# A chunked scan and a routed expert layer: every engine of the scan in a fixed order, routing in smaller groups

## The chip, the cores and the metric

The kernel runs on one core of one Trainium2 chip. A core has five engines that run side by side, each with an instruction queue of its own that it works through in order: PE (TensorE, matrix multiplies; PEld in the tables is its weight load), DVE (VectorE), ACT (ScalarE), POOL (GpSimd) and SP (SyncE, which here only issues transfers). The metric is the device time of one execution in microseconds; lower is better.

## The reference

Two blocks in a row. The first is a state-space scan over 4 batches, 8 heads and 768 positions (head width 32, state width 16); the second takes its output as 3072 tokens of width 256 and sends each to one of 8 experts.

```python
for c in range(nc):                       # along the sequence, per batch and head
    cum = np.cumsum(log(a_chunk)); L = exp(cum_i - cum_j) * causal
    y[chunk] = ((C @ B.T) * L) @ x + (C @ state) * exp(cum)
    state = exp(sum(log a)) * state + sum(B * x * exp(cum_last - cum))
x = y as (3072, 256)
logits = normalize(x) @ normalize(expert_emb).T / tau
e = argmax(logits);  gate = softmax(logits)[e]
out[token] = gate * (relu(x[token] @ w1[e]) @ w2[e])
```

## The kernel before

**Tiling.** The sequence is cut into 6 chunks (`c`) of 128 positions. A unit is one batch of one chunk (all 8 heads); two units make a **pair** `p`, so that there are 12 pairs, two for a chunk. The scan is a software pipeline over steps `i` from -2 to 13: step `i` prepares pair `i+2` (B' and its transpose, the scaled C), makes the masked products of pair `i` (`inner`), the outputs of pair `i-1` (`outputs_before` from the states, `outputs_within` from the products), and turns pair `i-2` into rows by token together with its logits (`finish`, `keep_tokens`).

**Decays.** `decays` computes running products of `a` for chunks 0 to 3 (`kk` = 0) and 4 to 5 (`kk` = 1), scales for C in `f` and for B in `r`; `turn_decays` transposes `r` to `rT`. `scale_b` makes B' (`bp`) for a whole chunk, `scale_c` makes `cp` (DVE) and its two masked copies `cm` (ACT). `between` gets the decay from one chunk to the next by a scan over all 768 positions of a second copy of `a`; `spread_between` lays it out by four small multiplies and makes `blocks`, from which POOL builds the state weights `T` (four a chunk).

**Routing.** For each chunk, four units at once, `pick` finds the best expert of every token (six small DVE operations on the logits in `yt`), `place` counts with ones-matrices on PE how many tokens came before and writes the row number `row_of`, and POOL sends the four units' rows to a table `rows` in DRAM by four indirect transfers (a **scatter**). The last 160 rows of each expert's window of 416 are filled with ones first, by eight transfers from `none`.

**Experts.** Afterwards `moe` loads each expert's 416 rows (`xg`, issued by SP once all scatters have landed), multiplies up (`hp`), down (`yp`), and scatters the results to the output. Weights have three buffers; the first three experts' weights are loaded during the scan.

**Order.** The order on PE is the order of the code. On the other four engines a planner sets it at build time, by readiness as it estimates it; so the constants, the fills and the scan of `between` stand early there.

```python
        with tc.manual_schedule(engines={PE}):
            build_consts(k)
            route_consts(k)
            mamba(k)
```

Of the kernel before, what the change touches and what calls it, by code (L numbers as in the profile page):

```python
# [15 lines left out]
PE = mybir.EngineType.PE  # L16
# [8 lines left out]
KD, KF = DM // 128, F // 128  # L25
TR, NT = 104, 4
# [19 lines left out]
def build_consts(k):  # L46
    nc, pool = k.nc, k.const
    k.ident = pool.tile([128, 128], F32, name="ident")
# [40 lines left out]
def load_decays(k):  # L89
# [8 lines left out]
    k.a1 = k.mc.tile([NB * NH, S], F32, name="a1")  # L98
    nc.scalar.dma_start(k.a1[:], a)


def clip(k, v):
    k.nc.vector.tensor_scalar(out=v, in0=v, scalar1=1e-6, scalar2=1.0, op0=ALU.max, op1=ALU.min)


def decays(k, kk):
# [4 lines left out]
    clip(k, a)  # L111
    at = k.mc.tile([128, 1], F32, name=f"at{kk}")
    nc.vector.tensor_copy(out=at[:], in_=a[:, HQ : HQ + 1])
    nc.vector.memset(a[:, 0:Q:HQ], 0.0)
    nc.vector.tensor_tensor_scan(out=f, data0=a, data1=k.heads[:], initial=0.0, op0=ALU.mult, op1=ALU.add)
    w = k.mc.tile([128, 2], F32, name=f"w{kk}")
    tt(out=w[:, 0:1], in0=f[:, HQ - 1 : HQ], in1=at[:], op=ALU.mult)
    nc.vector.reciprocal(out=w[:, 1:2], in_=w[:, 0:1])
    nc.vector.reciprocal(out=r, in_=f)
    nc.vector.tensor_scalar_mul(r[:, 0:HQ], r[:, 0:HQ], w[:, 0:1])  # L120
    nc.vector.tensor_scalar_mul(f[:, 0:HQ], f[:, 0:HQ], w[:, 1:2])
# [9 lines left out]

def between(k):

    nc = k.nc
    a = k.a1
    clip(k, a[:])
    at = k.mc.tile([NB * NH, NC], F32, name="at")
    nc.vector.tensor_copy(out=at[:], in_=a[:, HQ:S:Q])
    nc.vector.memset(a[:, HQ:S:Q], 0.0)
    one = k.mc.tile([NB * NH, S], F32, name="one")  # L140
    nc.vector.memset(one[:], 0.0)
    nc.vector.memset(one[:, HQ:S:Q], 1.0)
    p = k.mc.tile([NB * NH, S], F32, name="p")
    nc.vector.tensor_tensor_scan(out=p[:], data0=a[:], data1=one[:], initial=0.0, op0=ALU.mult, op1=ALU.add)
    k.g = k.mc.tile([NB * NH, NC - 1], F32, name="g")
    nc.vector.tensor_tensor(out=k.g[:], in0=p[:, Q + HQ - 1 : S : Q], in1=at[:, 1:], op=ALU.mult)


def spread_between(k):
# [15 lines left out]
def expert_emb(k):  # L165

    nc = k.nc
    k.en = k.mc.tile([E, DM], F32, name="emb")
    nc.scalar.dma_start(k.en[:], k.emb)
    tau = k.mc.tile([E, 1], F32, name="tau")  # L170
    nc.scalar.dma_start(tau[:], k.tau.to_broadcast([E, 1]))
    sq = k.mc.tile([E, DM], F32, name="emb_sq")
    r = k.mc.tile([E, 1], F32, name="emb_r")
    nc.scalar.activation(sq[:], k.en[:], ACT.Square, accum_out=r[:])
    nc.gpsimd.tensor_tensor(out=r[:], in0=r[:], in1=k.half[0:E, 0:1], op=ALU.pow)
    nc.vector.tensor_scalar_add(r[:], r[:], 1e-6)
    nc.vector.tensor_tensor(out=r[:], in0=r[:], in1=tau[:], op=ALU.mult)
    nc.vector.reciprocal(out=r[:], in_=r[:])
    nc.vector.tensor_scalar_mul(k.en[:], k.en[:], r[:])
# [327 lines left out]


def place(k, c):

    nc = k.nc
# [363 lines left out]
```

## Time and profile before

| | us |
|---|---|
| Time of three runs | 334.68, 338.02, 339.41; median 338.02 |
| Profiled execution: time | 335.96 |
| Profiled execution: span | 334.2 |
| Start to the first `inner` product | 0 to 25.98 |
| Then to the end of `outputs_within` of pair 1 | to 42.53 |
| Then to the end of `outputs_within` of pair 11 | to 106.33 |
| Then to the issue of the first expert's rows | to 119.58 |
| Experts | 119.58 to 334.2 |

The span runs from the first to the last instruction; the profiled execution's time is 1.76 us more than it. Instructions have a start, a length and, in brackets, how long their engine stood idle before them and which event ended that. "PEclk" in a table is the granted share of TensorE's clock, 1.00 being 2.4 GHz and 0.50 1.2 GHz.

### The profile page before, as it was taken

How to read it: one execution, taken by the hardware profiler on the slowest of the kernel's cores; microseconds unless marked ns; L12 is line 12 of the kernel's file. 1: busy time of each engine (PE TensorE's matmuls, PEld its weight loads, DVE VectorE, ACT ScalarE, POOL GpSimd, SP SyncE). 2: the span in 40 equal slices, each digit the busy share in tenths (PEclk: the TensorE clock that was granted, in tenths of full speed). 3: DMA queues.
4: the chain of work that ended last, by engine and by line, in shares of the span. 5: the costliest groups of instructions: out<-in, count | busy, mean ns of one | idle time of the engine just before them, and what ended most of it. 6: DMA issues, size and time to landing. Idle time of an engine off the chain costs nothing.

```text
span 334.2 us, 4458 instructions
## 1 busy us (share of the span) xinstructions
PE 278.9 (83%) x1687; PEld 173.4 (52%) x1687; DVE 125.7 (38%) x371; ACT 66.6 (20%) x177; POOL 86.0 (26%) x107
## 2 busy tenths in 40 slices
PE   0439999999877019999999999999999999999930
PEld 0235788668656015555555555555555555555510
DVE  7815777456540615214214214214224114123030
ACT  2012253224312016121121031031121001011000
POOL 8202314453340713013114014014014004013040
PEclk9999999799797757999999999999999999999985
DMA  6899824010110252234415414514523001001010
GB/s 210 307 361 338 325 69 128 35 56 16 69 50 20 100 142 54 70 112 151 142 63 158 170 28 160 185 34 143 180 69 106 0 0 43 2 0 51 0 40 14
DMA packets 17871, 35.09 MB, mean 105 GB/s; under 512 B 2054, under 2 KB 10451, under 8 KB 17848
## 3 DMA queue, kind: packets, MB, share of 16 engines
q1 hardware_dynamic: 14168, 26.74, 24.4%
q0 software_dynamic: 2688, 6.50, 6.2%
q10 hardware_dynamic: 992, 1.55, 1.2%
q8 instruction: 14, 0.23, 0.3%
q14 instruction: 9, 0.07, 0.1%
HBM read 26.89 MB, written 8.14 MB: 105 GB/s over the span
## 4 chain that ended last, share of the span: by engine, by line
PE 59%; issue 20%; DMA 11%; DVE 5%; POOL 1%; ACTq 1%; ACT 1%; POOLq 0%; SPq 0%; DVEq 0%
PE hp L626 19%; PE yp L640 17%; DMA out_dram<-yo,to 8%; PE pg L308 6%; PE pz L362 4%; PE py L344 2%; PE py L330 2%; PE pf L252 2%; DMA rows<-none 2%; PE xt L617 2%; PE ot L654 1%; PE pf L270 1%; POOL out_dram L657 1%; DMA xg<-rows 1%; DVE g L314 1%
## 5 line engine op out<-in xcount | busy, mean ns | idle before, releaser
L626 PE MATMUL hp<-xT,w 128*128 128x416 f32 x256 | 97.3, 521 | 0.0
L640 PE MATMUL yp<-hT,w 128*128 128x416 f32 x256 | 90.8, 513 | 0.0
L640 PEld LDWEIGHTS yp<-hT,w 128*128 128x128 f32 x256 | 48.1, 190 | 38.5 <-issue 38.5
L626 PEld LDWEIGHTS hp<-xT,w 128*128 128x128 f32 x256 | 47.2, 193 | 32.9 <-issue 31.6
L657 POOL DMA_INDIRECT out_dram<-yo,to x32 | 32.2, 1006 | 91.5 <-DVE yo L656 84.8
L632 DVE TENSOR_SCALAR hT<-hp 128x416 f32<-128x416 f32 x32 | 18.9, 591 | 40.7 <-PE hp L626 27.5
L630 ACT ACTIVATE hT<-hp 128x416 f32<-128x416 f32 x32 | 16.6, 518 | 84.1 <-PE hp L626 61.4
L537 POOL DMA_INDIRECT rows<-yt,row_of x24 | 23.4, 976 | 30.5 <-issue 21.1
L314 DVE TENSOR_TENSOR g<-pg,mask 128x1024 f32<-128x1024 f32 x24 | 28.2, 1219 | 6.5 <-PE pg L308 6.5
L596 POOL TENSOR_TENSOR gr<-gr,half 104x4 f32<-104x4 f32 x8 | 8.3, 1036 | 75.9 <-ACT sq L592 75.9
L291 POOL TENSOR_TENSOR T<-V,blocks 128x256 f32<-128x256 f32 x20 | 12.6, 653 | 41.0 <-DVE blocks L159 14.6
L308 PE MATMUL pg<-cm,bt 32*128 32x256 f32 x192 | 21.8, 479 | 1.2 <-issue 0.9
L362 PE MATMUL pz<-turn,yT 128*128 128x136 f32 x96 | 17.5, 336 | 5.9 <-ACT yT L354 5.9
L362 PEld LDWEIGHTS pz<-turn,yT 128*128 128x128 f32 x96 | 14.8, 229 | 10.2 <-ACT yT L354 7.0
L656 DVE TENSOR_SCALAR yo<-ot,gate 104x256 f32<-104x256 f32 x32 | 15.4, 480 | 11.5 <-PE ot L654 11.5
L617 PE MATMUL xt<-ident,xg 104*128 104x104 f32 x64 | 7.8, 269 | 13.3 <-DMA xg<-rows 13.3
L647 DVE COPY yoT<-yp 128x416 f32<-128x416 f32 x8 | 4.7, 592 | 36.8 <-PE yp L640 26.1
L592 ACT ACTIVATE sq<-xg 104x256 f32<-104x256 f32 x32 | 12.9, 404 | 17.9 <-DMA xg<-rows 17.7
L654 PEld LDWEIGHTS ot<-ident,yoT 128*104 128x104 f32 x64 | 6.9, 130 | 16.6 <-DVE yo L656 8.5
L308 PEld LDWEIGHTS pg<-cm,bt 32*128 32x128 f32 x192 | 13.3, 220 | 4.4 <-issue 3.8
L645 ACT COPY yoT<-yp 128x416 f32<-128x416 f32 x8 | 4.1, 506 | 56.9 <-PE yp L640 56.9
L584 DVE TENSOR_REDUCE gm<-xg 104x4 f32<-104x32 f32 x8 | 1.5, 182 | 37.0 <-DMA xg<-rows 37.0
(147 smaller groups left out, 236.9 us busy)
## 6 DMA issues: line engine op xcount, KB each, us to landing
w<-in_moe_w_dram SPq DMA_DIRECT2D x16, 1024.0 KB
xg<-rows SPq DMA_DIRECT2D x8, 442.0 KB
x<-in_x_dram SPq DMA_DIRECT2D x6, 512.0 KB
b<-in_B_dram SPq DMA_DIRECT2D x6, 256.0 KB
ct<-in_CT_dram SPq DMA_DIRECT2D x6, 256.0 KB
rows<-none ACTq DMA_DIRECT2D x8, 170.0 KB
out_dram<-yo,to POOLq DMA_INDIRECT x32
rows<-yt,row_of POOLq DMA_INDIRECT x24
```

Of the source, the lines that this page charges most:

```text
L308: nc.tensor.matmul(k.pg[:, q, 256 * i : 256 * i + 256], lhsT=s.bt[r, i, :], rhs=s.cm[r, i], start=True, stop=True, tile_position=(32 * q, 0),)
L314: nc.vector.tensor_tensor(out=g[:], in0=k.pg[:, :, 256 * i : 256 * i + 256].rearrange("p q (t i) -> p q t i", t=2), in1=k.mask[:].unsqueez ...
L362: k.nc.tensor.matmul(k.pz[:, i, at : at + Y1], lhsT=yT[:, 2 * i + j, :], rhs=k.turn[:, j, :], start=(j == 0), stop=(j == 1), skip_group_ch ...
L537: d = nc.gpsimd.indirect_dma_start(out=k.rows[:, :], out_offset=bass.IndirectOffsetOnAxis(ap=row[:, b : b + 1], axis=0), in_=k.yt[:, NB * ...
L592: nc.scalar.activation(sq[:], s.x[:, i, :].rearrange("p (j w) -> p j w", j=KD)[:, :, 0:128], ACT.Square, accum_out=r[:, i : i + 1],)
L617: nc.tensor.transpose(t[:, i, :], s.x[:, i, Y1 * j : Y1 * j + 128], k.ident[:tr, :tr])
L626: nc.tensor.matmul(t[:], lhsT=s.w1[:, j, 128 * f : 128 * f + 128], rhs=s.xT[:, j, :], start=(j == 0), stop=(j == KD - 1))
L630: nc.scalar.activation(s.hT[:, f, :], t[:], ACT.Relu)
L632: nc.vector.tensor_scalar_max(s.hT[:, f, :], t[:], 0.0)
L640: nc.tensor.matmul(t[:], lhsT=s.w2[:, f, 128 * j : 128 * j + 128], rhs=s.hT[:, f, :], start=(f == 0), stop=(f == KF - 1),)
L656: nc.vector.tensor_scalar_mul(y[:], t[:tr, :], s.gate[:, i : i + 1])
L657: d = nc.gpsimd.indirect_dma_start(out=k.out[:, :], out_offset=bass.IndirectOffsetOnAxis(ap=s.to[:, i : i + 1], axis=0), in_=y[:], in_offs ...
```

## The change

- All engines of the scan now follow the order of the code; constants and the routing constants get places in it (`build_consts` first, `route_consts` in step 1).
- The fills move from ACT's queue to SP's, into step 1; the loads of the first weights move from step 1 to step 2 and stand behind the chunk loads there.
- The expert embedding is finished in step 1 instead of step -1.
- B' is made for one pair at a time, at the end of the step before its use.
- The decay from chunk to chunk comes from columns that `decays` already has (`finish_decays`), and the scan over 768 positions, with its own copy of `a`, goes.
- The state update is four combined operations for a chunk instead of two, into a new buffer each time; POOL's `T` are issued as `next_states` at a later place, from 12 buffers instead of 8.
- Routing groups: chunks 0 to 2 stay whole, chunks 3 to 5 are routed by pair (nine groups instead of six). Counting carries a running row, so that a group needs 3 or 5 small multiplies on PE instead of 5 to 10.
- Scatters: tables say in which step which group is picked (`PICK`), located (`PLACE`) and scattered (`SCATTER`), mostly two transfers a step; a second half first copies one element of the outputs of pair `i-2`, the others set one element.

```diff
+GROUPS = [(c, 0, NB) for c in range(3)] + [(c, b, 2) for c in range(3, NC) for b in (0, 2)]
 def decays(k, kk):
...
+def finish_decays(k, kk):
+    nc.vector.reciprocal(out=w[:, 1:2], in_=w[:, 0:1])
+    nc.vector.tensor_scalar_mul(f[:, 0:HQ], f[:, 0:HQ], w[:, 1:2])
+    nc.vector.tensor_tensor(out=w[:, 2:3], in0=w[:, 0:1], in1=at[:, 0:1], op=ALU.mult)
+    nc.vector.tensor_scalar_mul(k.parts[:, 0, kk, :], k.block[:], f[:, Q - 1 : Q])
+    nc.vector.tensor_scalar_mul(k.parts[:, 1, kk, :], k.block[:], w[:, 2:3])
...
 def between(k):
-    nc.vector.tensor_tensor_scan(out=p[:], data0=a[:], data1=one[:], initial=0.0, op0=ALU.mult, op1=ALU.add)
...
+        nc.tensor.matmul(
+            ps[:, 16 * b : 16 * b + 16], lhsT=k.spread[:, b, :], rhs=k.parts[:].rearrange("p v k g -> p (v k g)"),
...
 def states(k, c):
+        nc.vector.scalar_tensor_tensor(
+            out=V[:, b, :], in0=k.V[c - 1][:, b, :], scalar=k.whole[:, b, c - 1 : c], in1=st[:, b, :], op0=ALU.mult,
+            op1=ALU.add,
+        )
...
+        if i == 1:
+            fill_rows(k)
+        if i in (2, 4, 7):
+            load_weights(k, len(k.w1t))
+        for g in PLACE.get(i, ()):
+            locate(k, g)
+        if new is not None:
+            scale_c(k, new)
+        if 0 <= i < NP:
+            inner(k, i)
+        for g, u, n in SCATTER.get(i, ()):
+            scatter(k, g, u, n, done)
+        if i == 1:
+            next_states(k, 0)
+        elif i % 2 == 0 and 2 <= i and i // 2 < NC - 1:
+            next_states(k, i // 2)
...
+        for g in PICK.get(i, ()):
+            pick(k, g)
+        if new is not None and new + 1 < NP:
+            scale_b(k, new + 1)
         if i == -1:
             decays(k, 1)
+            finish_decays(k, 1)
+        if i == 0:
+            turn_decays(k, 1)
+            between(k)
+        if i == 1:
             turn_emb(k)
-        if i == 1:
-            turn_decays(k, 1)
-        if i % 2 and i >= 3:
-            pick(k, (i - 3) // 2)
-    place(k, NC - 1)
+            route_consts(k)
+    last = len(GROUPS) - 1
+    locate(k, last)
+    scatter(k, last, 0, 2, None)
+    count(k)
+PICK = {4: [0], 6: [1], 7: [2], **{p + 2: [p - 3] for p in range(6, 12)}}
+PLACE = {5: [0], 7: [1], 8: [2], **{p + 3: [p - 3] for p in range(6, 11)}}
+SCATTER = {
+    5: [(0, 0, 2)], 6: [(0, 2, 2)], 7: [(1, 0, 2)], 8: [(1, 2, 2), (2, 0, 2)], 9: [(2, 2, 2), (3, 0, 2)],
+    **{p + 3: [(p - 3, 0, 2)] for p in range(7, 11)},
+}
+def scatter(k, g, first, n, behind):
+    for u in range(first, first + n):
+        if u == first > 0:
+            nc.gpsimd.tensor_copy(out=k.tick[:], in_=k.yT[behind][0:1, 0, 0:1])
+        else:
+            nc.gpsimd.memset(k.tick[:], 0.0)
+        d = nc.gpsimd.indirect_dma_start(
```

ACT's queue at the start, before (`emb_sq` prepares the embedding, `none` is the tile of ones that the fills write to `rows`).

```order
L174 ACT_TABLE_LOAD
L174 ACTIVATE emb_sq,emb_r<-emb 8x256
L129 COPY rT<-pz 128x128
L242 COPY bt<-pz 128x256
L483 DMA rows<-none 80x544 x8
L262 ACTIVATE cm<-cp,tmask 128x2x128 x2
```

ACT's queue at the same place, changed.

```order
L169 ACT_TABLE_LOAD
L169 ACTIVATE emb_sq,emb_r<-emb 8x256
L123 COPY rT<-pz 128x128
L260 ACTIVATE cm<-cp,tmask 128x2x128 x2
L240 COPY bt<-pz 128x256
```

The fills are gone from between the first transposed B' (`bt`) and the first masked copies (`cm`), and `cm` stands ahead of `bt`.

DVE's queue at the start, before: from the long scan of `between` to the first B' (each of the last two rows one chunk).

```order
L144 SCALAR_TENSOR_TENSOR p_229<-a1_180,one_226 32x768
L117 TENSOR_TENSOR w1_302<-f_168,at1_298 128x1
L119 RECIPROCAL r_169<-f_168 128x128
L146 TENSOR_TENSOR g_231<-p_229,at_223 32x5
L118 RECIPROCAL w1_302<-w1_302 128x1
L120 TENSOR_SCALAR r_169<-r_169,w1_302 128x64
L121 TENSOR_SCALAR f_168<-f_168,w1_302 128x64
L220 TENSOR_TENSOR bp_219<-b_183,rT_170 128x16x16 x2
L220 TENSOR_TENSOR bp_258<-b_202,rT_170 128x16x16 x2
```

DVE's queue, changed: the second set of decays (chunks 4 and 5, to `parts`), and what stands behind it, the scaled C of pair 2 and the first masked product.

```order
L109 MEMSET a0_135 128x2
L110 SCALAR_TENSOR_TENSOR f_85<-a0_135,heads_90 128x128
L112 TENSOR_TENSOR w1_238<-f_85,at1_234 128x1
L113 RECIPROCAL r_86<-f_85 128x128
L114 TENSOR_SCALAR r_86<-r_86,w1_238 128x64
L132 RECIPROCAL w1_238<-w1_238 128x1
L133 TENSOR_SCALAR f_85<-f_85,w1_238 128x64
L134 TENSOR_TENSOR w1_238<-w1_238,at1_234 128x1
L135 TENSOR_SCALAR parts_88<-block_119,f_85 128x4
L136 TENSOR_SCALAR parts_88<-block_119,w1_238 128x4
L255 TENSOR_TENSOR cp_255<-ct_156,pf_81 128x256
L320 TENSOR_TENSOR g_268<-pg_79,mask_128 128x1024
```

The second set of decays has moved from ahead of the first B' to behind the B' of three pairs, directly ahead of `cp` of pair 2 and `g` of pair 0; the long scan is gone.

POOL's queue in the scan, before: the first scatters of rows, the state weights `T` behind them, the next scatters.

```order
L537 DMA rows_57<-yt_128,row_of_640 24576x272 x4
L291 TENSOR_TENSOR T_699<-V_171,blocks_279 128x256
L291 TENSOR_TENSOR T_701<-V_171,blocks_279 128x256
L291 TENSOR_TENSOR T_703<-V_171,blocks_279 128x256
L291 TENSOR_TENSOR T_705<-V_171,blocks_279 128x256
L537 DMA rows_57<-yt_128,row_of_798 24576x272 x4
```

POOL's queue, changed: the first scatters, of the same chunk 0 (steps 5 and 6).

```order
L582 MEMSET tick_89 1x1
L583 DMA rows_57<-yt_133,row_of_650 24576x272
L582 MEMSET tick_89 1x1
L583 DMA rows_57<-yt_133,row_of_650 24576x272
L580 COPY tick_89<-yT_712 1x1
L583 DMA rows_57<-yt_133,row_of_650 24576x272
L582 MEMSET tick_89 1x1
L583 DMA rows_57<-yt_133,row_of_650 24576x272
L296 TENSOR_TENSOR T_745<-V_714,blocks_297 128x256
L296 TENSOR_TENSOR T_747<-V_714,blocks_297 128x256
L296 TENSOR_TENSOR T_749<-V_714,blocks_297 128x256
L296 TENSOR_TENSOR T_751<-V_714,blocks_297 128x256
```

The group of four is split in two by a copy from `yT`, and each scatter has a small operation on one element (`tick`) ahead of it.

## Rows read from the trace of the kernel before

**Rows 1.** Busy time by stage; after each engine's time its instruction count.

```profile
core 0: us, PE busy (x) PEld busy (x) DVE busy (x) ACT busy (x) POOL busy (x), PEclk, DMA share, GB/s
0.00:25.98 25.98, 6.98 (x54) 5.25 (x54) 15.22 (x67) 3.69 (x9) 10.46 (x25) 1.00 0.86 296
25.98:42.53 16.55, 16.31 (x187) 11.73 (x187) 10.21 (x14) 4.99 (x12) 4.04 (x7) 1.00 0.87 315
42.53:106.33 63.80, 56.80 (x778) 46.37 (x779) 34.80 (x77) 20.72 (x43) 23.29 (x28) 0.92 0.17 57
106.33:119.58 13.25, 2.06 (x35) 1.68 (x33) 6.01 (x33) 1.18 (x2) 7.72 (x8) 0.72 0.24 85
119.58:334.20 214.62, 196.73 (x640) 108.32 (x640) 59.42 (x180) 35.99 (x112) 40.49 (x40) 0.95 0.26 81
```

**Rows 2.** The chain that ended last, in order of time, from 14 us.

```profile
14.28 6.98 DMA rows<-none
```

**Rows 3.** Timeline of the start: start, length, engine, instruction, idle before and releaser.

```profile
7.95 0.58 POOL L175 TENSOR_TENSOR emb_r<-emb_r,half 8x1 f32<-8x1 f32 x1
8.12 0.27 ACT L129 COPY rT<-pz 128x128 f32<-128x128 f32 x1 [1.54 <-PE pz L128]
8.49 1.89 DVE L144 TENSOR_TENSOR_SCAN p<-a,one 32x768 f32<-32x768 f32 x1
11.71 1.43 DVE L220 TENSOR_TENSOR bp<-b,rT 128x256 f32<-128x256 f32 x4
...
13.37 7.83 ACTq L483 DMA_DIRECT2D rows<-none  x8
...
14.16 0.34 DVE L179 TENSOR_SCALAR emb<-emb,emb_r 8x256 f32<-8x256 f32 x1
...
15.04 0.42 DVE L257 TENSOR_TENSOR cp<-ct,pf 128x256 f32<-128x256 f32 x1 [0.54 <-PE pf L252]
...
21.25 0.91 ACT L262 ACTIVATE cm<-cp,tmask 128x256 f32<-128x256 f32 x2 [7.58 <-DMA rows<-none]
...
22.47 1.86 PE L155 MATMUL pz<-g,spread 32*128 32x5 f32 x8 [6.26 <-ACT bt L242]
...
25.06 2.34 POOL L291 TENSOR_TENSOR T<-V,blocks 128x256 f32<-128x256 f32 x4 [14.59 <-DVE blocks L159]
...
28.25 2.36 DVE L314 TENSOR_TENSOR g<-pg,mask 128x1024 f32<-128x1024 f32 x2 [0.32 <-PE pg L308]
```

**Rows 4.** Timeline of PE, the products of `outputs_within` of five pairs.

```profile
33.81 1.93 PE L344 MATMUL py<-g,x 128*32 128x128 f32 x32
...
46.44 1.06 PE L344 MATMUL py<-g,x 128*32 128x128 f32 x32
51.41 1.06 PE L344 MATMUL py<-g,x 128*32 128x128 f32 x32
56.81 1.41 PE L344 MATMUL py<-g,x 128*32 128x128 f32 x32
65.96 1.06 PE L344 MATMUL py<-g,x 128*32 128x128 f32 x32
```

**Rows 5.** Timeline at the first burst of scatters: POOL's last, and ACT's next copy.

```profile
59.05 0.96 POOL L537 DMA_INDIRECT rows<-yt,row_of  x1 [0.30 <-DVE bp L220]
...
61.04 0.58 ACT L354 COPY yT<-py 128x512 f32<-128x512 f32 x1 [4.39 <-remote]
```

**Rows 6.** Busy time in a stretch behind a burst, columns as in rows 1.

```profile
61.04:64.45 3.41, 3.41 (x18) 2.67 (x15) 2.30 (x4) 1.39 (x3) 0.19 (x1) 0.50 0.01 2
```

**Rows 7.** Timeline of the tail of the scan.

```profile
108.96 0.18 DVE L494 TENSOR_REDUCE m<-yt 128x4 f32<-128x32 f32 x1 [1.59 <-ACT yt L370]
...
111.45 0.17 DVE L535 CAST row_of<-m 128x4 int32<-128x4 f32 x1
...
117.01 0.96 POOL L537 DMA_INDIRECT rows<-yt,row_of  x1 [0.30 <-issue]
...
119.58 6.39 SPq L565 DMA_DIRECT2D xg<-rows  x3
```

More of the change, by code (lines that the diff above doesn't have):

```diff
@@ L376, in mamba @@
     k.rT = k.mc.tile([128, 2, 128], F32, name="rT")
[L377 to L378 removed]
+    k.parts = k.mc.tile([128, 2, 2, 4], F32, name="parts")
+    k.tick = k.mc.tile([1, 1], F32, name="tick")
+    k.T, k.V, k.yT, k.dec, k.to = {}, {}, {}, {}, {}
+    NP = NU // 2
+    build_consts(k)
     load_decays(k)
     load(k, 0)
+    load_emb(k)
+    load(k, 1)
     decays(k, 0)
     turn_decays(k, 0)
[L383 to L384 removed]
+    finish_decays(k, 0)
     scale_b(k, 0)
[L386 removed]
@@ new lines, in mamba @@
+        if done is not None:
+            finish(k, done)
+        if new is not None:
+            turn_b(k, new)
+        if done is not None:
+            keep_tokens(k, done)
+        if new is not None:
+            keep_b(k, new)
+        if out is not None:
+            outputs_before(k, out)
+        if new is not None and c < NC - 1:
+            sums(k, new)
+        if out is not None:
+            outputs_within(k, out)
+            keep_outputs(k, out)
+        if new is not None and i % 2 and c < NC - 1:
+            states(k, c)
@@ L509, in place, with locate @@
-def place(k, c):
+        nc.vector.reduce_sum(
+            out=k.ob[:, g + 1, 0, :], in_=k.ob[:, g, 0 : nb + 1, :].rearrange("p u e -> p e u"), axis=AX.X
+        )
+def locate(k, g):
     nc = k.nc
     w = k.work
-    ob = k.ob.pop(c)
-    at = k.pz[:, 1, 392 : 392 + NB * E].rearrange("p (b e) -> p b e", b=NB)
-    terms = [(k.before, ob[:], at)]
-    for v in [k.first[:]] + [k.sums[:, i, :] for i in range(c)]:
-        terms.append((k.ones, v.unsqueeze(1).to_broadcast([128, NB, E]), at))
-    for i in range(NB - 1):
-        terms.append((k.ones, ob[:, i : i + 1, :].to_broadcast([128, NB - 1 - i, E]), at[:, i + 1 :, :]))
-    for i, (lhsT, rhs, out) in enumerate(terms):
+    c, b, nb = GROUPS[g]
+    at = k.pz[:, 1, 392 : 392 + nb * E].rearrange("p (b e) -> p b e", b=nb)
+    ob = k.ob[:, g, 1 : nb + 1, :]
+    nc.tensor.matmul(at, lhsT=k.before[:], rhs=ob, start=True, stop=False, skip_group_check=True)
+    for i in range(nb):
@@ L822 @@
         k.pz = ps.tile([128, 2, 512], F32, name="pz")
-        with tc.manual_schedule(engines={PE}):
-            build_consts(k)
-            route_consts(k)
+        with tc.manual_schedule():
             mamba(k)
```

249 lines of the change are left out of this document (109 added, 140 removed).

## The prediction

> **What bounds the kernel now.** I read the table by stage first. In [rows 1] the experts take 214.62 of 334.2 us, and the diff touches none of their operations, so the whole change is in the first 119.58 us. Those fall into four stretches with different limits, and each has to be asked which wait ends last in it.
>
> In the first stretch (25.98 us) PE is busy for 6.98 us only; it waits. The chain of waits passes through 6.98 us of the fills [rows 2], and the timeline shows why [rows 3]: ACT's queue holds eight fills from 13.37 on, 7.83 us long, and the masked copies `cm`, whose input `cp` is ready at 15.04 + 0.42 = 15.46, start only at 21.25, with an idle time of 7.58 us put down to `rows<-none`. PE's four multiplies for the decay between chunks start at 22.47 behind ACT's `bt` (idle 6.26), so `blocks` and the first `T` (25.06) are late as well. Ahead of that DVE is the bound: `rT` is ready at 8.12 + 0.27 = 8.39, but the first `bp` starts at 11.71, behind the scan of 1.89 and the rest of the second set of decays.
>
> In the loop (63.80 us) the spacing of `outputs_within` tells the rhythm [rows 4]: 46.44 to 51.41 is 4.97 for a plain step, 56.81 to 65.96 is 9.15 for one with a burst of scatters. In such a step POOL's last scatter starts at 59.05, and ACT's copy of the outputs at 61.04 after 4.39 us of idle time put down to "remote" [rows 5]: the products themselves are short (1.41 at 56.81), only their completion arrives 2.0 us after the last scatter's start. Behind it lies a stretch at half clock, 0.50 over 3.41 us [rows 6]. The eight steps up to pair 11 take 53.9 us, 8 x 4.97 = 39.8; with four bursts in them that is 14.1 / 4 = 3.5 us for a burst.
>
> In the tail (13.25 us) everything is serial [rows 7]: outputs end at 106.33, the pick starts at 108.96, the row numbers are done at 111.62, the last of a queue of eight scatters starts at 117.01, and the experts' rows are issued 2.57 later.
>
> **The change part by part.** The sum is made against the profiled execution: span 334.2, time 335.96, which lies 2.1 below the median of 338.02.
>
> *Start.* Three things go from it: the fills from ACT's queue, the 1.89 scan, and the second set of decays from ahead of `bp`. The first `bp` then follows `rT`: between 7.3 and 8.39, I take 7.9. A B' of one pair is two operations of half width. The four of [rows 3] took 1.43, 0.36 each, so one of half width costs between 0.18 and 0.36; I take 0.28, halfway up and more, since a cast of 128x4 still takes 0.17 [rows 7], so 0.56 a pair. But the fixed order puts the second decays directly ahead of `cp` of pair 2 and `g` of pair 0. They take at least the 1.43 us that followed the scan before (8.49 + 1.89 to 11.71, less the 0.1 overlap), and at most about 3.9 with `finish_decays` and the part that lay ahead of the scan; I take 3.4. On DVE this gives 7.9 + 3 x 0.56 (B') + 4 x 0.42 (`cp` three times, V) + 3.4 + 1.4 of waits for PE between them = 16.0 for the first `g` (28.25 before), done at 18.4. PE's multiplies for `between` (1.86) come in at about 17.5 to 19.8, two small DVE operations behind them end at 20.6, against 24.97 before. `T` of 2.34 follows, then the products at half clock (1.93 [rows 4]) and their copy: outputs of pair 0 end at about 25.2, where they ended at 35.74.
>
> Then comes something new. The embedding is finished in step 1, and POOL has it behind the four `T`: raising to a power (0.58), DVE's scaling (0.34 and three small ones), two transpositions and copies. Behind those stand ten DVE operations of `route_consts` ahead of `cp` of the next pair. It costs nothing if POOL is early, and at most about 4 us (2.34 + 0.58 + 1.1) if nothing is beside it; I take 1.9 for the embedding and 1.1 for the constants, 3.0. Step 2 I leave as it was, 6.8 (35.74 to 42.53). So the second stretch ends at 25.2 + 3.0 + 6.9 = 35.1 instead of 42.53: **-7.4**, between -10.5 (no such wait, full clock by 30) and 0 (everything given back). The weights' load in step 2 and the fills on SP's queue lie behind the loads of chunks 0 to 3; what they are queued ahead of, chunks 4 and 5 and later weights, is used twelve us and more later.
>
> Here the trace can be weighed against the notes. The row shows the fills holding ACT's own queue for 7.83 us with `cm` behind them [rows 3]. The Trainium skill, "DMA: Bandwidth & Descriptors", section "Issuing engines are not separate DMA queues", speaks against moving them: all issuers share the same 16 engines, and another issuer saves sequencer time that is "usually small relative to the DMA itself". By that only DVE's part of the gain (11.71 to 7.9, 3.8 us) would be left and the time would be 320.4; I go by the row, since what was lost there is ACT's time, not the transfers'.
>
> *Loop, ten steps, 63.80 us.* Without its four bursts it is 63.80 - 14.1 = 49.7. Added on DVE: a pick per pair from chunk 3 on, and a state update of four operations. Four operations on 64 elements cost between 0.42 (the rate of `cp`'s 256) and 4 x 0.42 = 1.7; I take 0.85, which is what the two before took. New is that PE's `locate` opens a step, ahead of `cp`'s spread and `inner`, and waits there for the pick that closed the step before, in odd steps behind V's four operations and once behind a long chain. Nothing, if DVE (busy 34.80 of 63.80 [rows 1]) has caught up; at most a whole pick (six operations from 108.96 on [rows 7], 1.33) in eight steps, 10.6. I take 0.5 in four steps, **+2.0**, near the lower end by DVE's share.
>
> The scatters: a burst of four had its last start 3 x 1.26 after its first (0.96 + 0.30 [rows 5]) and released PE 2.0 later, 5.8 in all. A pair with a `tick` in each gap (0 to 0.30, I take 0.13) releases at 1.4 + 2.0 = 3.4 after its first start. That takes 2.4 of the 3.5, leaving 1.1 at most if a pair begins as late in its step as a burst did; nothing if it is over before the products are due. The first halves begin early in the step, behind the row numbers; the second halves behind the copy of the outputs before, at which PE has just finished such products. I take 0.5 on the mean of eight steps, two of them with four scatters: **+4.1**. The bounds are 0 and 28 (8 x 3.5). The loop then is 49.7 + 2.0 + 4.1 = 55.8, **-8.0**.
>
> *Tail.* The last group is a pair: outputs to pick 2.5 (2.63 before), pick to row numbers 2.3 (2.66), first scatter 0.75 behind, second 1.4 behind it, experts' rows 2.57 behind that: 9.5 against 13.25, **-3.75**. Six fewer scatters in the last queue carry it; bounds -2.5 and -5.
>
> *The rest at nothing:* `T` from twelve buffers (POOL is busy 23.29 of 63.80), counting with fewer multiplies (PE is not the bound in a plain step by more than 0.3), the count of rows after the last scatter, which lies beside its 2.57 of landing.
>
> Sum: 335.96 - 7.4 - 8.0 - 3.75 = 316.8, say **317**.
>
> **Rivals.**
> A (slower): each pair of scatters holds PE as long as a burst did. What counts would then be that a scatter is in flight when products end, not how many. For it speaks that the release followed the last scatter by the same 2.0 us in all four bursts; against it, that a plain step shows no hold at all and a pair's release comes 2.4 earlier. Price 8 x 3.5 = 28 instead of 4.1: 341. It turns the result round from 3.1 us a step on (317 - 4.1 + 25 = 338).
> B: the start gives its gain back. The second stretch ends at 42.5 again, because `g` and `between` wait in the fixed order of DVE, or because weights and fills (DMA share 0.87 before [rows 1]) delay a chunk: 335.96 - 8.0 - 3.75 = 324.
> C: pairs cost nothing and the start runs at full clock from 30 on: 317 - 4.1 - 2 = 311.
> D: DVE becomes the bound of the routing steps. With `g` 2.36, a pick 1.33, `locate`'s 0.68, B' 0.56, `cp` 0.42 and V 0.85 behind each other at 6.2 and 0.4 of waits a step of 6.6 results, 1.4 over my mean in seven steps: 327.
> E: B and D together, or the planner's order had hidden all of it already: 334.
>
> **How the numbers follow.** The forecast has 0.52 (312 to 322), C 0.15, B 0.13, D 0.09, E 0.05, A 0.06. A run of this kernel tells a change from none at about 2%, that is below 331.3 or above 344.8. Faster are the forecast, B, C and D, less a little of D: 0.87; A and E lie mostly within 2% (0.09), and A with the longer bursts of steps 8 and 9 dearer still may lie above it (0.04). The range reaches from just below C with its bound at the start, 307, over B and D to 328; it leaves out A, E and the ends.
>
> **What would show it.** In the changed profile: `cm` follows `cp` on ACT at once, with no idle time put down to `rows<-none` (fills); the first `bp` starts at 7.3 to 8.4; `g` at about 16; an idle time of PE of about 2 us ahead of the embedding's transpositions, which would be the new wait; outputs of pair 1 end near 35. In the loop the spacing of the products lies at 5.0 to 5.5, up to 6.2 in the steps with four scatters, and ACT's idle time ahead of `yT` stays under 3.4. The experts' rows are issued 9.5 behind the last outputs. I am wrong if ACT's copies still wait 4 us at each pair (A), if the second stretch ends at 40 or later (B), or if the experts' 214.62 move by more than 1 us, which nothing here foresees.

## The result and the profile after

The changed kernel takes 318.67 us (median of four runs, 315.9 to 319.87), the kernel before 338.72 on the same chip: ratio 0.943, 95% interval 0.932 to 0.955. The forecast was 317, within 307 to 328. The profiled execution is the fastest of the four, 315.9, with a span of 314.1.

The sets of runs in this study fell on different chips, and the kernel before does not take the same time on them: 338.7 us where the result was measured (called the first chip here; whether it is the same as the second isn't known), 333.4 on the second, 318 to 319 on the third and on the fourth. So each ratio is to the kernel before in the same set, and stages are compared across chips only where the text says so. The changed kernel itself ran on the first and the third chip alone.

The table by stage, columns as in [rows 1]; the stretches end at the first `inner`, at the end of `outputs_within` of pairs 1 and 11, and at the issue of the experts' rows.

```profile
0.00:13.16 13.16, 5.17 (x47) 3.49 (x47) 8.25 (x38) 4.38 (x10) 5.90 (x15) 1.00 0.75 258
13.16:31.99 18.83, 15.90 (x200) 12.03 (x200) 16.00 (x51) 5.08 (x12) 6.43 (x16) 0.82 0.45 152
31.99:89.82 57.83, 51.31 (x775) 43.55 (x776) 41.87 (x118) 20.02 (x41) 28.68 (x52) 0.94 0.53 184
89.82:99.89 10.07, 1.75 (x16) 1.23 (x15) 6.14 (x34) 1.18 (x2) 4.46 (x9) 0.79 0.19 69
99.89:314.10 214.21, 196.65 (x640) 108.26 (x640) 59.53 (x180) 35.98 (x112) 40.48 (x40) 0.95 0.27 81
```

Three stretches have become shorter: the start by 10.5 (42.53 to 31.99), the loop by 6.0 (63.80 to 57.83), the tail by 3.2 (13.25 to 10.07); the experts have not moved. DVE is busier in the loop than before (41.87 in 57.83 against 34.80 in 63.80).

The timeline of the start.

```profile
8.13 0.49 DVE L224 TENSOR_TENSOR bp<-b,rT 128x128 f32<-128x128 f32 x2 [0.23 <-ACT rT L123]
...
12.68 6.04 SPq L521 DMA_DIRECT2D rows<-none  x8
...
16.61 2.35 DVE L320 TENSOR_TENSOR g<-pg,mask 128x1024 f32<-128x1024 f32 x2
...
20.74 2.33 POOL L296 TENSOR_TENSOR T<-V,blocks 128x256 f32<-128x256 f32 x4 [13.80 <-DVE blocks L155]
...
26.26 0.20 PE L187 MATMUL pz<-ident,emb 8*128 8x8 f32 x1 [1.84 <-DVE emb L181]
```

It went as the sum had it: B' at 8.13 (forecast 7.9, in [rows 3] 11.71), the first `g` at 16.61 (16.0), `T` at 20.74 (20.6), and the new wait of PE for the embedding, 1.84. The fills are 6.04 us of SP's queue now, and nothing on the way waits for them.

PE's products of pairs 0, 1, 6, 7 and 8, as in [rows 4].

```profile
22.70 1.72 PE L350 MATMUL py<-g,x 128*32 128x128 f32 x32
...
30.94 1.05 PE L350 MATMUL py<-g,x 128*32 128x128 f32 x32
...
58.31 1.06 PE L350 MATMUL py<-g,x 128*32 128x128 f32 x32
...
64.49 1.11 PE L350 MATMUL py<-g,x 128*32 128x128 f32 x21
66.63 0.64 PE L350 MATMUL py<-g,x 128*32 128x128 f32 x11 [1.03 <-issue]
...
75.68 1.08 PE L350 MATMUL py<-g,x 128*32 128x128 f32 x32
```

From products to products the four steps behind pair 1 take 5.0 to 5.8, the one that ends at 58.31 takes 6.3, and in the two with four scatters lies the rest: 58.31 to 64.49, 6.2, and 64.49 to 75.68, 11.2. There the pattern of [rows 5] is back, POOL's last scatter of four and ACT's next copy:

```profile
64.69 0.96 POOL L583 DMA_INDIRECT rows<-yt,row_of  x1 [0.21 <-issue]
...
66.67 0.60 ACT L376 COPY yt<-pz 128x528 f32<-128x528 f32 x1 [3.61 <-remote]
```

The release comes 2.0 us behind the scatter's start, as before. In the stretch 70 to 74 the granted clock is 0.50, as in [rows 6].

The tail, as in [rows 7]: the queue of scatters at its end has two instead of eight.

```profile
95.88 0.96 POOL L583 DMA_INDIRECT rows<-yt,row_of  x1 [1.51 <-issue]
...
97.15 1.13 POOL L583 DMA_INDIRECT rows<-yt,row_of  x1 [0.23 <-issue]
...
99.89 0.81 SPq L619 DMA_DIRECT2D xg<-rows  x2
```

### The profile page after: what moved, and what is told of

It is laid out like the page before. It is cut to its first block, busy times and chain, and to the rows that moved or that the text cites. A ratio compares the mean times of both kernels' runs of the same rounds, so it can differ in the third digit from the quotient of the medians.

```text
span 314.1 us, 4507 instructions
## 1 busy us (share of the span) xinstructions
PE 270.8 (86%) x1670; PEld 168.6 (54%) x1670; DVE 131.8 (42%) x419; ACT 66.6 (21%) x177; POOL 86.0 (27%) x131
## 4 chain that ended last, share of the span: by engine, by line
PE 58%; issue 16%; DMA 11%; DVE 9%; ACT 2%; POOL 1%; another core or an unknown queue 1%; ACTq 0%; POOLq 0%; DVEq 0%; SPq 0%
PE hp L680 20%; PE yp L694 18%; DMA out_dram<-yo,to 8%; PE pg L314 4%; PE pz L368 4%; DVE g L320 3%; PE pf L250 2%; PE py L336 2%; PE ot L708 2%; PE py L350 1%; PE xt L671 1%; DMA xg<-rows 1%; PE pf L268 1%; POOL out_dram L711 1%
## 5 line engine op out<-in xcount | busy, mean ns | idle before, releaser
L314 PE MATMUL pg<-cm,bt 32*128 32x256 f32 x192 | 20.6, 448 | 0.0
L368 PE MATMUL pz<-turn,yT 128*128 128x136 f32 x96 | 16.3, 319 | 1.8 <-ACT yT L360 1.4
L296 POOL TENSOR_TENSOR T<-V,blocks 128x256 f32<-128x256 f32 x20 | 11.7, 618 | 20.1 <-DVE blocks L155 13.8
L368 PEld LDWEIGHTS pz<-turn,yT 128*128 128x128 f32 x96 | 13.6, 213 | 5.8 <-issue 3.3
L260 ACT ACTIVATE cm<-cp,tmask 128x256 f32<-128x256 f32 x24 | 10.9, 500 | 22.6 <-DVE cp L255 20.5
```

The lines of the kernel that those rows point to most:

```text
L314: nc.tensor.matmul(k.pg[:, q, 256 * i : 256 * i + 256], lhsT=s.bt[r, i, :], rhs=s.cm[r, i], start=True, stop=True, tile_position=(32 * q, 0),)
L368: k.nc.tensor.matmul(k.pz[:, i, at : at + Y1], lhsT=yT[:, 2 * i + j, :], rhs=k.turn[:, j, :], start=(j == 0), stop=(j == 1), skip_group_ch ...
```

## The experiments

**Fills alone (second chip).** In the kernel before, only the issuing engine of the fills is changed. (The planner then also starts them earlier, at 8.40 instead of 13.37, so that the run tests both together.)

```diff
     for e in range(E):
-        nc.scalar.dma_start(
+        nc.sync.dma_start(
             k.rows[T * e + CAP - FILL : T * e + CAP, :].rearrange("(p t) w -> p (t w)", p=80), none[:]
```

> The kernel before with one edit: the eight fills are issued by SP instead of ACT. If the fills cost what they hold ACT's queue (theory of the prediction): cm starts at about 15.5 instead of 21.25, PE's multiplies for the decay between chunks 5 to 6 us earlier, outputs of pair 1 end near 37 instead of 42.53, time 332 to 334 against 338.7. If the issuing engine hardly matters because the transfers share the same DMA engines (rival): within 1 us of 338.7.

326.47 against 333.38: ratio 0.975 (0.969 to 0.982). The masked copies follow `cp` at once, the multiplies of `between` too:

```profile
15.93 0.91 ACT L262 ACTIVATE cm<-cp,tmask 128x256 f32<-128x256 f32 x2
...
16.14 1.87 PE L155 MATMUL pz<-g,spread 32*128 32x5 f32 x8
...
33.55 1.06 PE L344 MATMUL py<-g,x 128*32 128x128 f32 x32
```

They stand at 21.25 and 22.47 in [rows 3], and the products of pair 1 end at 34.61 instead of 42.53 on the first chip. So this one word of the change, with the earlier place that it brought, is worth 6.9 us; 5 to 7 were expected.

**Fills back on ACT (second chip).** The reverse edit in the changed kernel.

```diff
     for e in range(E):
-        nc.sync.dma_start(
+        nc.scalar.dma_start(
```

> The changed kernel with one edit: the eight fills go back to ACT's queue, at their place in step 1. Theory: ACT is held 6 to 8 us with cm and bt of the next pairs behind it, outputs of pair 1 end 4 to 6 us later than 31.99, time about 323 to 325 against 318.7. Rival (issuer hardly matters): within 1 us of 318.7.

315.11, ratio 0.944 (0.940 to 0.948). The changed kernel did not run on this chip; against its 0.943 on the first no loss is seen. The wait exists, but the trace shows it covered:

```profile
18.52 5.01 ACTq L521 DMA_DIRECT2D rows<-none  x8
...
23.63 0.91 ACT L260 ACTIVATE cm<-cp,tmask 128x256 f32<-128x256 f32 x2 [4.91 <-DMA rows<-none]
...
28.11 0.20 PE L187 MATMUL pz<-ident,emb 8*128 8x8 f32 x1 [1.62 <-DVE emb L181]
```

`cm` waits 4.91 us, and PE waits for the embedding all the same; the products of pair 1 start at 32.19, within the 31.2 to 33.9 of the later runs with the fills on SP. So it is the place in the order that paid, behind the first pairs' copies; at that later place the issuer shows no effect. My expectation of 4 to 6 us fell. The loop of this run (33.88 to 89.68) takes 55.80 us, that of the kernel before with its fills on SP, on the same chip, 63.83 (34.61 to 98.44).

**Scatters one pair a step (second chip).** Only the table; the last three pairs go to step 13.

```diff
-    7: [(1, 0, 2)], 8: [(1, 2, 2), (2, 0, 2)], 9: [(2, 2, 2), (3, 0, 2)],
-    **{p + 3: [(p - 3, 0, 2)] for p in range(7, 11)},
+    7: [(1, 0, 2)], 8: [(1, 2, 2)], 9: [(2, 0, 2)], 10: [(2, 2, 2)],
+    11: [(3, 0, 2)], 12: [(4, 0, 2)], 13: [(5, 0, 2), (6, 0, 2), (7, 0, 2)],
```

> The changed kernel with only the table of scatters changed: one pair in each of the steps 5 to 12, three pairs in step 13 where no more outputs are made, one in the tail; no step up to 12 has four. Theory (four scatters reach into the column-tiled products and hold them, a pair does not): the products of pairs 6, 7, 8 lie 5 to 5.5 apart instead of 6.2 and 11.2, about 6.5 less, with 1 to 2 more in the tail: 313.5 to 315 against 318.7. Rival (those two steps are long through the chain from pick to locate on DVE, which stays): less than 1 us gained, and the tail's loss on top: 318.5 to 320.5.

322.87, ratio 0.965 (0.960 to 0.971): slower than the run with the fills on ACT in the same set (315.11), whose table is that of the changed kernel. The table did not do what I meant. The second half of group 2 waits for a copy of outputs, and the two pairs behind it, whose row numbers are long known, then follow it in a row: six starts from 78.56 on. The last of them and ACT's next copy:

```profile
84.92 0.96 POOL L583 DMA_INDIRECT rows<-yt,row_of  x1 [0.22 <-issue]
...
87.12 0.59 ACT L360 COPY yT<-py 128x512 f32<-128x512 f32 x1 [7.07 <-remote]
```

Again 2.2 us behind the last start, after 7.07 us of waiting; that step takes 11.3 (80.23 to 91.57). In the steps before that row ACT's copies wait less than 2 us. So this row of six holds PE longer than rows of four do, and single pairs hold it little: the step up to pair 5, with one pair, takes 5.72 here and 5.22 on the third chip. The expected gain did not show, so the run leaves open what a table without such a row would give on this chip.

**Without the copy ahead of second halves (second chip).**

```diff
-        if u == first > 0:
-            nc.gpsimd.tensor_copy(out=k.tick[:], in_=k.yT[behind][0:1, 0, 0:1])
-        else:
-            nc.gpsimd.memset(k.tick[:], 0.0)
+        nc.gpsimd.memset(k.tick[:], 0.0)
```

> The changed kernel with the second halves no longer held behind the copy of outputs: a memset takes its place, the order on POOL is the same. Theory: the pairs of steps 5 and 6 run together as four, and those of 7 and 8, each costs about 3.5 us as the bursts of the kernel before did, with half clock behind: 324 to 327 against 318.7. Rival (a scatter costs the same wherever it stands, or the hold came from the count of scatters in all): within 1 us of 318.7.

319.81, ratio 0.956 (0.949 to 0.964). In the same set the run with the fills on ACT, which has the copy, takes 315.11. Of these 4.7 us 1.7 lie ahead of the products of pair 1 (33.93 against 32.19), where the copy plays no part yet. From the start of pair 1's products to that of pair 11's it is 57.75 against 56.41 (57.80 for the changed kernel on the first chip, 30.94 to 88.74): 1.3 us at most. Pairs do run together as four, and the release follows again (51.70, then ACT's copy at 53.63), but what a step loses the next one mostly gets back: the steps up to pairs 5 and 6 are 7.0 and 5.2 instead of 5.7 and 6.3, those up to pairs 7 and 8 10.9 and 5.5 instead of 6.2 and 9.3. So a burst of four is not worth 3.5 us in this kernel, where the step behind it can win most of it back. My expectation of that size fell, and the copy as a gate gained 1.3 us at most. What keeps the hold small in this loop is not shown by it: with rows of four the loop takes 57.33 here, and that of the kernel before 63.83.

**The changed kernel on the third chip.**

> The changed kernel itself, on the chip of this set, as its base: ratio 0.94 to 0.95. Its products of pair 1 start at 30.9 if PE runs the start at full clock as in the first profile, at 33.9 if it runs it at half clock as in the two later variants with the same start.

316.09, but the kernel before takes 318.82 there: ratio 0.986 (0.978 to 0.995). The gain is 1.4% instead of 5.7%. Its products of pair 1 start at 33.94.

**The kernel before on the third chip.**

> The kernel before itself, for its trace on the chip of this set, since its time went from 338.7 on the first chip to 333.4 and 318.8 on the two others while the changed kernel stayed at 315 to 319. Theory: what differs between the chips is the hold of PE's products by scatters in flight. Where this kernel takes about 319, its steps with a burst of four scatters are 5 to 6 long instead of 9.15 and ACT's copies wait under 2 us there; its start (outputs of pair 1 end near 42.5) and its tail (13.25) are the same on every chip. Rival: the start is shorter there, because its loads arrive earlier, and the bursts are as long as on the first chip.

318.45, ratio 1.001. Its stages, columns as in [rows 1]:

```profile
24.30:40.79 16.49, 14.02 (x192) 10.30 (x192) 10.98 (x18) 5.20 (x12) 4.96 (x8) 0.90 0.96 336
40.79:89.28 48.49, 47.72 (x780) 40.89 (x780) 34.75 (x77) 21.04 (x43) 23.38 (x28) 1.00 0.24 82
89.28:102.52 13.24, 2.06 (x33) 1.68 (x33) 6.26 (x33) 1.19 (x2) 7.71 (x8) 0.69 0.24 85
```

The same instructions take 48.49 in the loop instead of 63.80, with PE busy for 47.72 of it. The first burst of scatters stands there as it did, and nothing is held (POOL's last scatter of the four, the next copy of ACT, the products around them):

```profile
55.07 1.06 PE L344 MATMUL py<-g,x 128*32 128x128 f32 x32
...
57.41 0.96 POOL L537 DMA_INDIRECT rows<-yt,row_of  x1 [0.30 <-issue]
...
60.05 1.06 PE L344 MATMUL py<-g,x 128*32 128x128 f32 x32
61.22 0.59 ACT L354 COPY yT<-py 128x512 f32<-128x512 f32 x1 [1.34 <-PE py L344]
```

The step takes 4.98 where [rows 4] have 9.15. Of the ten steps from the products of pair 1 to those of pair 11 the four with a burst are 4.2, 2.8, 3.7 and 4.6 us shorter than on the first chip, and the other six agree within 0.01. The start is 1.7 shorter (40.79), the tail the same (13.24). So the theory held: the chips differ in the hold. By stage, in us:

| | before, 1st chip | changed, 1st | before, 3rd chip | changed, 3rd |
|---|---|---|---|---|
| to the end of pair 1's outputs | 42.53 | 31.99 | 40.79 | 35.29 |
| to the end of pair 11's outputs | 63.80 | 57.83 | 48.49 | 55.23 |
| to the experts' rows | 13.25 | 10.07 | 13.24 | 9.28 |
| experts | 214.62 | 214.21 | 214.28 | 214.30 |

Without the hold the change makes the loop longer, by 6.7 us. Where these lie the changed kernel's trace on this chip shows (POOL, DVE's `pick`, PE's `locate` and `finish`):

```profile
54.41 2.34 POOL L296 TENSOR_TENSOR T<-V,blocks 128x256 f32<-128x256 f32 x4
...
54.96 1.29 DVE L535 TENSOR_TENSOR oh<-yt,m 128x32 f32<-128x32 f32 x1
...
56.28 0.53 DVE L538 TENSOR_TENSOR oh<-oh,rank 128x32 f32<-128x32 f32 x1
...
57.32 0.19 PE L560 MATMUL pz<-ob,before_b 128*128 128x32 bf16 x1 [1.46 <-DVE ob L542]
...
59.54 2.18 PE L368 MATMUL pz<-turn,yT 128*128 128x136 f32 x8
```

`pick` runs beside `T`, two of its operations take 1.29 and 0.53 instead of 0.19, PE waits 1.46 at the head of the step for its last results, and the products behind that wait run at the lower level (2.18 for `finish`, 1.19 in other steps; granted clock 0.53 in 60 to 62). That step is 8.3 long (54.80 to 63.14), the next two 6.2 and 6.95; the other seven are 4.0 to 5.3. What the lower level costs in it can be read from another run on this chip, that with chunk 5 whole (below): the same step there has the same wait of 1.46, but PE stays at the upper level (columns as in [rows 1], first this run, then that one).

```profile
54.80:63.14 8.34, 6.88 (x106) 5.82 (x98) 6.08 (x15) 2.37 (x5) 4.03 (x8) 0.80 0.90 329
...
52.31:59.01 6.70, 5.24 (x105) 4.50 (x98) 6.04 (x15) 2.37 (x5) 4.03 (x8) 1.00 1.05 391
```

So 1.6 of the 8.3 us are the clock, and of the 6.7 that remain DVE is busy for 6.0.

**Each pair gated, one pair a step (third chip).** The table of the run with one pair a step on the second chip, and the copy ahead of every pair.

```diff
-        if u == first > 0:
+        if u == first and behind is not None:
```

> The changed kernel with one pair of scatters in each of the steps 5 to 12 (three in step 13), as in the run called spread, but every pair is held behind the copy of the outputs two steps back, so that none can start ahead of its step and no two pairs run together before step 13. Theory (a pair at the start of its step costs nothing, scatters that run on into the column-tiled products hold them): products of pairs 5 to 11 lie 4.3 to 6.3 apart, none over 6.5; from the products of pair 1 to those of pair 11 about 51 to 53 instead of 57.8. Rival (the long steps come from PE's wait for pick ahead of locate and from the half clock behind such a wait): still one or two steps of 8 and more, 56 to 58.

314.7, ratio 0.990 (0.987 to 0.994): as the changed kernel. The loop takes 52.04, but the tail 13.21, as six scatters stand at its head. From the products of pair 1 to those of pair 11 it is 52.0, as the theory had it (51 to 53) and not the rival (56 to 58); but the chip shows no hold, so this run can't judge that theory. The steps of 6.7 and 6.2 that remain carry waits of PE for `pick` (1.44 and 1.17), the rival's cause, at the upper level of the clock.

**Scatters late (third chip, two sets).**

```diff
-    5: [(0, 0, 2)], 6: [(0, 2, 2)], 7: [(1, 0, 2)], 8: [(1, 2, 2), (2, 0, 2)], 9: [(2, 2, 2), (3, 0, 2)],
-    **{p + 3: [(p - 3, 0, 2)] for p in range(7, 11)},
+    13: [(0, 0, 4), (1, 0, 4), (2, 0, 4)] + [(g, 0, 2) for g in range(3, 8)],
...
-    k.to[g] = w.tile([128, NB], I32, name="row_of", tag="row_of", bufs=4)
+    k.to[g] = w.tile([128, NB], I32, name="row_of", tag="row_of", bufs=9)
```

> The changed kernel with all scatters but the last pair moved to step 13, behind the last products: the loop without any scatter, with all its picks and locates. From the products of pair 1 to those of pair 11: 50 to 52 instead of 57.8 if the scatters cost what is above a plain step; 56 or more if it is the chain from pick to locate. The 22 scatters then stand in a row at the end, 22 x 1.27 = 28 less what the tail had: the whole time is 12 to 18 us longer, 330 to 336.

> The changed kernel with all scatters but the last pair ungated and behind the last state weights (as in the run called late_scatters, whose trace showed 22 of them in one row from 61.9 on, beside the products of pairs 7 to 11). Theory: on a chip that holds the products behind scatters (before at 331 to 340) each of those five steps is held until the row of scatters ends, and the time is over 325; on a chip that doesn't (before at about 319) it is 312 again. Rival (the hold belongs to the kernel and not to the chip): 312 on every chip.

311.99 and 312.44, ratio 0.980 and 0.981. The first expectation missed by 20 us: POOL runs through its list as soon as row numbers are there, so 20 scatters stood in a row from 61.92 to 86.2, beside the products of pairs 7 to 11, instead of behind them. As a loop without scatters it failed; instead it shows that on this chip twenty in a row hold nothing: ahead of pair 7 there is one step of 8.7, with `T` from 59.37 on beside `pick` (7.1 in the second set, where PE stays at the upper level), and the products behind it lie 4.9, 4.5, 4.7 and 4.0 apart. The second set fell on the same chip, so that what the row costs where scatters hold PE was not seen.

**Chunk 5 whole in the tail (third chip).** The tables lose the group that this takes away.

```diff
-GROUPS = [(c, 0, NB) for c in range(3)] + [(c, b, 2) for c in range(3, NC) for b in (0, 2)]
+GROUPS = [(c, 0, NB) for c in range(3)] + [(c, b, 2) for c in range(3, NC - 1) for b in (0, 2)] + [(NC - 1, 0, NB)]
```

> The changed kernel with chunk 5 routed whole again (one group of four in the tail instead of two pairs). Theory: two scatters more at the end, 2.5, and a wider pick and locate, 0.2 to 0.4: from the end of the last products to the issue of the experts' rows 12.5 to 13 instead of 10.07. In return step 12 and 13 lose a pick and a locate, 0 to 1 earlier. The time is 1.5 to 3 us longer. Rival (the queue of scatters was not the tail's limit): no difference in that stretch.

The tail takes 12.08 instead of 9.28: 2.8 more, as expected. The time, 315.01 (0.989), doesn't show it, since in the profiled execution the start was 3.0 and the loop 1.1 shorter.

**Locate a step later (fourth chip).** Both tables.

```diff
-PLACE = {5: [0], 7: [1], 8: [2], **{p + 3: [p - 3] for p in range(6, 11)}}
+PLACE = {5: [0], 8: [1], 9: [2], 10: [3], 11: [4], 12: [5], 13: [6, 7]}
...
+    5: [(0, 0, 2)], 6: [(0, 2, 2)], 8: [(1, 0, 2)], 9: [(1, 2, 2), (2, 0, 2)], 10: [(2, 2, 2), (3, 0, 2)],
+    11: [(4, 0, 2)], 12: [(5, 0, 2)], 13: [(6, 0, 2), (7, 0, 2)],
```

> The changed kernel with only the tables changed: every locate behind the first stands one step later, a whole step behind its pick, and the scatters follow (two steps with four, 9 and 10, as the changed kernel has in 8 and 9). Theory (PE waits at the head of a step for a pick that DVE has just made, and a stretch at half clock follows such a wait): the waits of 1.0 to 2.0 us ahead of locate go, and the products of pairs 5 to 8, which lay 8.3, 6.2 and 6.9 apart on the chip without a hold, lie 5 to 5.5 apart: 4 to 5 us less from the products of pair 1 to those of pair 11 there (about 51 instead of 55.5), time 311 to 312 where the kernel before takes 318. On a chip with the hold the two steps with four scatters stay long and 2 to 4 us are gained. Rival (the steps are long for DVE's work itself, which stays): no change, 316.

310.82 against 318.81, ratio 0.974 (0.968 to 0.981). The changed kernel did not run on this chip; on the third, where the kernel before takes the same time, it has 0.986 (0.978 to 0.995). Products of pairs 5 to 8 and the `locate` between them:

```profile
53.34 1.06 PE L350 MATMUL py<-g,x 128*32 128x128 f32 x32
58.31 1.06 PE L350 MATMUL py<-g,x 128*32 128x128 f32 x32
59.30 0.19 PE L560 MATMUL pz<-ob,before_b 128*128 128x32 bf16 x1
63.92 1.08 PE L350 MATMUL py<-g,x 128*32 128x128 f32 x32
64.94 0.19 PE L560 MATMUL pz<-ob,before_b 128*128 128x32 bf16 x1
...
68.25 1.17 PE L368 MATMUL pz<-turn,yT 128*128 128x136 f32 x8 [1.53 <-DVE oh L567]
...
70.46 1.08 PE L350 MATMUL py<-g,x 128*32 128x128 f32 x32
```

Up to pair 11 no `locate` has an idle time of PE ahead of it. The loop takes 50.08 (55.23 for the changed kernel on the third chip, 1.6 of it the half clock in one step), with the granted clock at 1.00; the tail takes 10.47 instead of 9.28. In the one step of 6.5 that is left `pick` runs beside `T`, DVE is busy for 6.30 us of it, and PE waits 1.53 for DVE ahead of `finish` (the line at 68.25): there the rival, DVE's work itself, is right. The tables move the scatters too, and this alone shortens the way from the products of pair 1 to those of pair 11: 50.2 here, 52.0 with each pair gated, 52.6 and 51.6 with the scatters late, 55.5 in the changed kernel. So of the 5.3 us gained there only 1.4 to 2.4 can be put down to `locate` alone.

**`T` ahead of the scatters (fourth chip).** `next_states` is called before `scatter` in a step instead of behind it.

> The changed kernel with one edit: in each step POOL builds the state weights T ahead of the scatters instead of behind them. In the traces so far a small operation of pick that runs beside T takes 0.5 to 1.55 us instead of 0.19. Theory (T beside pick stretches pick and with it PE's wait): no operation of pick over 0.3 us, PE's wait ahead of locate in steps 7 and 9 shorter by 1 to 1.5, 2 to 4 us less from the products of pair 1 to those of pair 11 on a chip without a hold; where scatters hold the products, their start 2.3 later in even steps takes that back. Rival (pick was stretched by something else, such as the transfers): the same long operations, no change.

311.9, ratio 0.978 (0.973 to 0.983). In step 6 `T` is over before `pick` begins, in step 8 it is not:

```profile
48.82 2.43 POOL L296 TENSOR_TENSOR T<-V,blocks 128x256 f32<-128x256 f32 x4 [0.26 <-DVE V L285]
...
59.31 2.34 POOL L296 TENSOR_TENSOR T<-V,blocks 128x256 f32<-128x256 f32 x4 [1.23 <-DVE V L285]
```

```profile
54.43 0.19 PE L560 MATMUL pz<-ob,before_b 128*128 128x32 bf16 x1
...
61.75 0.19 PE L560 MATMUL pz<-ob,before_b 128*128 128x32 bf16 x1 [2.07 <-DVE ob L542]
```

Behind the first no operation of `pick` is over 0.3 us, though a scatter runs beside it (52.86 to 53.83), PE doesn't wait, and the step takes 5.3 (53.34 to 58.62). Beside the second three operations of `pick` take 0.62, 0.54 and 0.32, PE waits 2.07 and runs at the lower level behind it (`finish` 2.02), and the step takes 8.7 (58.62 to 67.35). So both halves of the chain are shown in one trace: `T` beside `pick` stretches it, and PE pays. The loop takes 52.68, 2.5 less than that of the changed kernel on the third chip.

## Why the prediction came out

**The start, forecast -7.4, measured -10.5.** The steps held to a few tenths up to `T`: B' 8.13, `g` 16.61, `T` 20.74; the outputs of pair 0 end at 24.42 (25.2). From there to the end of pair 1's outputs it is 7.57, where the sum had 9.9: 3.0 for the embedding and the constants, and 6.9 (the step is 6.79) for "Step 2 I leave as it was". Less a plain step of 4.97, the embedding and the constants cost 2.6; so the mis-sized term is the step. In the kernel before PE ran most of it at the lower level (`finish` 1.82 at 39.25, where a plain step has 1.19); here it ran a part of it at the upper one. The 0.8 ahead of it is mostly the clock too: PE's multiplies for the decay between chunks, which I had at 1.86, took 1.03 in this execution (first line; the second is the changed kernel on the third chip).

```profile
18.72 1.03 PE L146 MATMUL pz<-parts,spread 128*128 128x16 f32 x8 [0.45 <-ACT rT L123]
...
18.86 1.86 PE L146 MATMUL pz<-parts,spread 128*128 128x16 f32 x8 [0.45 <-ACT rT L123]
```

That was luck: in all nine later profiles with the same code up to there they take 1.86, `T` starts at 21.7, and the products of pair 0 start at 24.55 to 24.57 instead of 22.70. Those of pair 1 start in eight of them at 32.6 to 33.9, 1.7 to 3.0 later than here, and in one at 31.2; with them -7.4 would have been near. This execution is the fastest of its four, the others are 2 to 4 us longer. That the fills' issuer weighs was right for the kernel before (7 us, with the earlier place). The rule of the Trainium skill, "DMA: Bandwidth & Descriptors", "Issuing engines are not separate DMA queues", against which I went, says that another issuer saves only sequencer time, usually little beside the transfer; the run at the later place agrees, where ACT's wait of 4.91 us was covered.

**The loop, forecast -8.0, measured -6.0.** Its three terms can be checked by the third chip, which has no hold. The first, 49.7 without the bursts, was worked out from held steps, and the kernel before takes 48.49 there: 15.3 us of hold. The second, +4.1 for the scatters that remain (0.5 in each of eight steps is 4.0), measures about 4.8, step by step against the third chip: 4.2 in the step up to pair 8 (11.2 against 6.95; 9.3 on the second chip), the half clock behind the hold included, and 0.6 in that up to pair 5 (5.78 against 5.22). So the change takes some 10.5 us of hold out of the loop, half of the whole gain on the first chip. Whether the shorter rows do that or their place in the step, no run separates. The size was right, the places were not: not 0.5 in each of eight steps, but nearly all of it behind four in a row. The term that failed is the third, +2.0 for `locate` behind `pick`: what is left on the first chip is 57.83 - 48.49 - 4.8 = 4.5, and the third shows 6.7. PE's waits ahead of `locate` alone add up to 4.4 on the first chip (1.01, 1.17, 1.46 and twice 0.36) and to 5.3 on the third. I had the wait in its place (the head of a step, behind `pick`) and its upper bound at 10.6, but took the lower end "by DVE's share", which says nothing of a wait at one point; and I left out that `T` beside `pick` stretches it and that PE may run at the lower level behind the wait, which is 1.6 of the third chip's 6.7. The errors, 1.2 too much in the first term, 0.7 and 2.5 too little in the others, make the 2.0; with the start's 3.1 and the experts' 0.4 of the other sign and the tail's 0.6 the sum of 316.8 came out at 315.9. That it came so near is partly luck: two errors of 2 to 3 us cancelled.

**The tail, forecast -3.75, measured -3.2** (-4.0 on the third chip). Right in its mechanism; the chunk as a whole in its place costs 2.8, near 2 x 1.27.

**The rivals.** A fell: no step with one pair is held for 3.5 us. B fell with the start, which ends at 31.99 and not at 42.5, and E with B; of C the start came true in this one execution. D, DVE as the bound, was nearer the truth than its chance: on the third chip DVE is busy for 6.0 of 6.7 us (without the half clock), 5.3 of 6.2 and 6.5 of 6.95 in the steps up to pairs 6 to 8, near the 6.6 that D had for a step, but in three steps and not in seven. What no rival had is that the result depends on the chip. On the third the same change is worth 1.4%, start -5.5 and tail -4.0 against a loop 6.7 longer. What makes one chip hold these products and another not, and whether it is the chip or a condition that lasts over a set, stays open: no run took a cause away, the sets with the hold were also the first ones in time, and the row of twenty scatters could not be tried on a chip that holds.

## What to carry to other kernels

An issue of transfers in a compute engine's queue can cost what stands behind it; moving it a few steps later can be worth as much as moving it to another engine. Where a step opens with a wait for the last result of the step before, price the wait by the chain that ends in it, not by the busy share of the engine that runs it, and give such a result a whole step of time. Before a gain is put down to an order, run the kernel before on a second chip: here it loses 15 us to a hold that another chip does not show, the change takes some 10 of these away, and the gain shrinks from 5.7 to 1.4% where there is none.

## What the runs showed of the hardware

**Chips differ.** The same kernel takes 338.7 and 318.5 us on two chips of one kind, with the experts equal within 0.4 us. Of the 17.4 us between the two profiled executions 15.2 are in the four steps with a burst of scatters, 9.15 against 4.98 for the first of them, and 1.7 in the start. Whether it is the chip or the time of the set that differs is open, as said of the rivals.

**DVE beside POOL.** With `T` on POOL, operations of `pick` that read two tensors took up to 1.76 us instead of 0.19 (in the changed kernel with the fills on ACT, at 67.71), and up to 0.62 directly ahead of `T`; those with one input stayed at 0.16 to 0.23. Two neighbours from the changed kernel on the third chip, where `T` runs from 70.50 to 72.83:

```profile
70.50 2.33 POOL L296 TENSOR_TENSOR T<-V,blocks 128x256 f32<-128x256 f32 x4
...
70.55 0.17 DVE L541 TENSOR_REDUCE m<-oh 128x2 f32<-128x16 f32 x1
70.75 1.55 DVE L542 TENSOR_TENSOR ob<-oh,m 128x16 bf16<-128x16 f32 x1
```

The Trainium skill, "GPSIMD Engine Reference", section "Specifications", says that GpSimd shares its SBUF interfaces with VectorE and contends with its instructions of two SBUF inputs; this trace agrees, and shows that it is DVE that pays here: `T` takes 2.33 to 2.37 beside `pick` and 2.33 at 20.74 without it.

**Granted clock and speed.** In the start on the third chip the records give a granted clock of 1.00 from 13.16 to 35.29, yet the products of pair 0 took 1.93 us, as at the lower level; the durations are the better witness there.
